# A given order of TensorE steps, loads and score sessions, two pairs a transposing bank, and one float of each row of w_in read into a scratch tile

## The chip, the core and the metric

The kernel runs on one NeuronCore of a Trainium2 chip. The metric is the device time of one execution in microseconds; the time before is the median of three runs. A profile of one further execution, taken by the hardware profiler, gives the spans of instructions on the five engines (PE is TensorE, DVE VectorE, ACT ScalarE, POOL GpSimd, SP SyncE), the landings of DMAs and the clock that PE was granted.

## What is computed

Causal attention over 4 batches, 8 heads, 768 positions and head size 64, followed by a gated feed-forward product. Three heads (0, 2 and 6) see all earlier positions; the five others see the first four positions (sinks) and a window of 64.

```python
scores = scale * np.matmul(q, k.transpose(0, 1, 3, 2))
causal = rel >= 0
is_sink = pos[None, :] < int(n_sink)
in_win = (rel >= 0) & (rel < int(window))
stream_keep = causal & (is_sink | in_win)
...
a = a / (np.sum(a, axis=-1, keepdims=True) + 1e-09)
return np.matmul(a, v).astype(np.float32)
...
x = np.ascontiguousarray(attn_out.transpose(0, 2, 1, 3)).reshape(B * S, H * D)
...
h = x @ w_in
g = h * (1.0 / (1.0 + np.exp(-beta * h)))
return (g @ w_out).astype(np.float32)
```

x has 3072 rows of 512, w_in is 512 x 2048, w_out is 2048 x 512; inputs and output are float32, the products run in bf16.

## The kernel before

The rows are cut into eight chunks of 384: chunk 2b is the first half of batch b, chunk 2b + 1 the second. A chunk goes through these steps, named as the planner names them:

- **Loads** (`load_hw`, `load_sw`, `load_v`, `load_rows`). K, Q and V of a chunk. Two loads each on SP and ACT bring the first heads of chunk 0 as float32; all others, and w_in and w_out in four pieces each, go through POOL's queue, which casts to bf16. `ORDER` names the order of the loads of w_in, w_out and chunks 1 and 2 behind those of chunk 0 ("k1a" is K of chunk 1, heads 0 to 3, "b" heads 4 to 7, "v10" a third of V of chunk 1).
- **Transposes of K and Q**. For chunks 0 to 2 (`BY_HAND_C = 3`) PE transposes them (`keys_ramp`, L542), one pair of heads to a PSUM bank, and DVE or ACT copies the bank to KT or QT (`copy`, L385). From chunk 3 on SP issues DMA transposes (`keys_rows`, L556).
- **Scores** in sessions (`session`, L689). A session fills some banks with blocks of 128 x 128; two heads run side by side in the upper and lower 64 rows of the array. ACT then takes the exponential of each bank into es (L698). Chunk 0's masks are added on PE as products with the identity (L674); the other chunks' masks are multiplied in on DVE (L718, L722). Copies of K and V blocks for the sinks (KO, VO) are made on POOL or DVE.
- **Probabilities times V** (L742), the reciprocal of the sums (L745) and the division into x (L752), all four pairs of heads.
- **Transposes of x** (`x_transposed`): on PE for chunks 0 to 3 and 7 (L764), with a copy to xT by DVE or ACT; as four DMA transposes on SP (L770) for chunks 4, 5 and 6.
- **First product** (`first_part`, L784): 16 groups of four matmuls of 384 columns, xT against w_in; ACT takes the tanh (th, L787) and DVE makes gT from it (gate, L789). A group's bank is held until DVE has read it.
- **Second product** (`second_part`, L804): three row tiles of 16 matmuls of 512 columns, gT against w_out; ACT or DVE copies the bank out (osb) and SP stores it. The last row tile is cut into two halves of 256 columns, each copied and stored in two quarters.

There are eight PSUM banks for all of it. All instructions are emitted by a planner (`Plan.run`), which replays the kernel with assumed costs and takes, on each engine, the task that can start first; the table of PE's lanes ("F1" first product, "F2" second product, "S" sessions) sets the order of these on PE, and all other PE tasks go ahead of them when ready. Before, that table came from `STAGE_0` for chunk 0 and from the function `stage`, which spreads both products evenly between sessions. Every engine executes its instructions in the order in which they were emitted. `fill` puts matmuls of zeros (L968) into waits of PE in the first 16 us of the plan; eight more (L448) stand at the very beginning.

Of the kernel before, what the change touches and what calls it, by code (L numbers as in the profile page):

```python
# [8 lines left out]
F32 = mybir.dt.float32  # L9
# [46 lines left out]
class Task:  # L56
    __slots__ = ("name", "alts", "deps", "prio", "emit", "take", "drop", "mode", "load", "n_wait", "after",
                 "done", "start", "engine", "seq", "follow", "lane")
# [11 lines left out]
class Rings:  # L70


    LAND = 1100.0

# [5 lines left out]
    def add(self, queue, task, ready, work, packet):  # L80
        self.queues[queue].append([task, ready, work, packet])

    def step(self, until):
# [11 lines left out]
        for q in self.queues.values():  # L95
            if q and q[0] in live and q[0][2] <= 1e-3:
                h = q.pop(0)
                self.landing.append((self.now + self.LAND, h[0].seq, h[0]))
                self.landing.sort()
# [19 lines left out]
class Plan:  # L119
# [6 lines left out]
    PATIENCE = 150.0  # L126

# [11 lines left out]
    def run(self, key, ahead):  # L139
# [48 lines left out]
        while left:  # L188
# [65 lines left out]
            t.start, t.engine = now, e  # L254
# [4 lines left out]
            if t.load is not None:  # L259
                kind, delay, work, packet = t.load  # L260
                rings.add(e, t, now + delay, work, packet)
# [19 lines left out]
    def let_go(self, h, at):  # L281
        h.users -= 1
        h.until = max(h.until, at)
        if h.users == 0:
# [7 lines left out]
FILL_END, FILL_SPARE = 16000.0, 120.0  # L292
BY_HAND_C = 3
AHEAD = 8
STAGE_0 = [(3, 0, 0), (3, 0, 1), (3, 0, 2), (3, 0, 3), (4, 0, None)]
SESSIONS = {0: [(3, 3), (3, 3)], 1: [(4, 3), (4, 3), (3, 3)]}
SESSIONS_1 = [(3, 2), (3, 2), (3, 3), (2, 2)]
# [4 lines left out]
def XT_PE(c, m):  # L302
    return c < 4 or c == 7
# [3 lines left out]
def kernel(  # L307
# [13 lines left out]
    nc = tc.nc  # L321
# [131 lines left out]
    PACKET = {256: 18.3, 768: 37.0, 2048: 78.0, 512: 27.0}  # L453
    seq, chain = [0], []

    def dma(name, queue, issue, size, count, deps, fn, take=(), drop=(), prio=None, follow=()):
# [3 lines left out]
        if queue == "POOL":  # L460
            follow, chain[:] = list(follow) + chain, []
        delay = issue + 700.0 if queue == "POOL" else max(issue, 460.0) + 640.0
        t = P.add(name, [(queue, issue, 0.0)], deps, seq[0] * 0.001 + (prio or 0), lambda _: fn(eng[queue]), take, drop,
                  load=(kind, delay, PACKET[size] * count, PACKET[size]), follow=follow)
# [68 lines left out]
    def keys_ramp(c, p):  # L533
        for name, holder, made in (("k", KH, GK), ("q", QH, GQ)):
            src = [QK[name, c, h] for h in PAIR[c][p]]
            bank = Hold(BANKS)

            def tr(_, bank=bank, src=src):
                tp = bank.buf.bitcast(BF16)[:, 0:HALF].rearrange("p (t j) -> p t j", t=HT)
                for t in range(HT):  # L540
                    for a, (_, hold, i) in enumerate(src):
                        nc.tensor.transpose(tp[half(a), t, :], hold.buf[:, i, t], ident)  # L542
            t = P.add(f"T{name}{c}.{p}", [pe(384, 3)], [x[0] for x in src] + [t_id], c * 100 + p * 10, tr, take=[bank], drop=[x[1] for x in src])

            def ev(e, bank=bank, holder=holder):
                tp = bank.buf.bitcast(BF16)[:, 0:HALF].rearrange("p (t j) -> p j t", t=HT)
                copy(e, holder[c].buf[:, p].rearrange("p (j t) -> p j t", t=HT), tp)
            made[c, p] = [P.add(f"E{name}{c}.{p}", [dve(384), act(384)] if c or p < 2 else [dve(384)], [t], c * 100 + p, ev, take=[holder[c]], drop=[bank])]
# [102 lines left out]
    def session(c, parts, prio, lane):  # L651
# [13 lines left out]
        by_pe = c == 0  # L665
# [11 lines left out]
        def go(_):  # L677
# [12 lines left out]
            for a, lo, part, bank in work if by_pe else []:  # L690
                if not retr[part[0][0]] and len(part) == 2:
                    nc.tensor.matmul(bank.buf[0:sink_i, 0:128], KH[f].buf[half(a), WHERE[c][part[0][0]][1], 0:sink_i], QH[c].buf[half(a), WHERE[c][part[0][0]][1], 256:384], start=True, stop=True)  # L692
        occ = max(time) / 2.4 + 5.0 * count + (sum(time) / 2.4 + 97.0 if by_pe else 0.0)
# [10 lines left out]
    def masks_and_products(c, pairs):  # L704
# [3 lines left out]
        for h in range(H):  # L708
            at, lst = PLACE[c, h]
            if c == 0:  # L710
                made[h] = []
                continue
            prio = c * 100 + 10 * WHERE[c][h][1] + 1
# [298 lines left out]
```

## Time and profile before

| | |
|---|---|
| runs | 234.52 us median (233.3, 234.52, 235.13) |
| the profiled execution | 234.75 us; span from its first to its last instruction 232.8 us |
| granted PE clock, mean | 0.991 |
| busy: PE, ACT, DVE, POOL | 221.4, 151.9, 142.0, 92.0 us |
| first product, 512 matmuls | 94.7 us busy |
| second product, records of 379 of its 400 matmuls | 89.0 us busy |
| tanh on ACT, 128 | 74.6 us busy |
| exponentials on ACT, 132 | 61.3 us busy |
| DMA | 25.77 MB in 92488 packets; POOL's queue 72.0% of 16 engines' span |

A row of the groups names the line, engine and operation, what it writes and reads, and the count; then the busy time in us and the mean ns of one; then the engine's idle time ahead of them and what ended it. The chain that ended last is followed back from the last instruction, at each step to what released it or to the instruction before it on its engine. In the table of stages each engine has its busy time and, in brackets, its instructions. Matmuls are pipelined, so the duration of one exceeds the distance from one to the next; the distance is what PE pays.

### The profile page before, as it was taken

To read this page: it belongs to the slowest core of one execution; us is meant where nothing else is said; L and a number is where in the kernel's file an instruction comes from. 1 tells how busy PE (TensorE), PEld (TensorE's weight loads), DVE (VectorE), ACT (ScalarE), POOL (GpSimd) and SP (SyncE) were. 2 spreads that over 40 slices of the span, in tenths; PEclk is the share of its full clock that TensorE was granted. 3 is DMA by queue.
4 is the path that set the end of the run, shared out by engine and by line. 5 is a ranking of instruction groups with operands and counts; after the bars stand their busy time and mean duration, and the time that the engine had idled before them with its cause. 6 is when DMAs were issued, how large, how long until landed. Compare 5 with 4: busy or idle time off the path is not lost.

```text
span 232.8 us, 5227 instructions
## 1 busy us (share of the span) xinstructions
PE 221.4 (95%) x1967; PEld 127.1 (55%) x1988; DVE 142.0 (61%) x353; ACT 151.9 (65%) x299; POOL 92.0 (40%) x141
## 2 busy tenths in 40 slices
PE   7999689999599999999999999999999999999993
PEld 3465466545365565655555556555655656555453
DVE  5666598655795666876775466674847458434321
ACT  3767998526569687776667876965676876555300
POOL 8948543698999834898600004100000000000000
PEclk9999999999799999999999999999999999999999
DMA  7999999999999999999992114311220110111112
GB/s 168 162 197 204 182 207 196 137 128 170 157 157 164 155 196 111 132 139 136 196 167 68 48 34 114 82 28 55 62 62 3 45 48 1 45 47 46 45 45 90
DMA packets 92488, 25.77 MB, mean 111 GB/s; under 512 B 83872, under 2 KB 89520, under 8 KB 92464
## 3 DMA queue, kind: packets, MB, share of 16 engines
q0 software_dynamic: 66144, 13.24, 72.0%
q1 hardware_dynamic: 25456, 11.67, 23.3%
q10 hardware_dynamic: 864, 0.53, 0.7%
q8 instruction: 15, 0.25, 0.4%
q14 instruction: 9, 0.07, 0.1%
HBM read 27.27 MB, written 6.29 MB: 144 GB/s over the span
## 4 chain that ended last, share of the span: by engine, by line
PE 90%; ACT 4%; DVE 3%; issue 1%
PE bank L804 36%; PE bank L784 35%; PE bank L689 6%; PE bank L742 5%; ACT es L698 4%; PE bank L542 2%; PE bank L764 2%; PE bank L448 2%; PE bank L674 1%; PE bank L968 1%; DVE gT L789 1%; DVE es L722 1%; DVE x L752 0%; PE bank L692 0%; DVE KO L385 0%
## 5 line engine op out<-in xcount | busy, mean ns | idle before, releaser
L787 ACT ACTIVATE th<-bank,beta_h 128x384 f32<-128x384 f32 x128 | 74.6, 592 | 40.9 <-PE bank L784 34.6
L784 PE MATMUL bank<-xT,w_in_sb 128*128 128x384 bf16 x512 | 94.7, 328 | 0.1
L804 PE MATMUL bank<-w_out_sb,gT 128*128 128x512 bf16 (+1 forms) x379 | 89.0, 372 | 1.4 <-issue 0.3
L789 DVE SCALAR_TENSOR_TENSOR gT<-th,bank 128x384 bf16<-128x384 f32 x128 | 69.3, 549 | 27.8 <-ACT th L787 24.5
L698 ACT ACTIVATE es<-bank 128x512 bf16<-128x512 f32 (+3 forms) x132 | 61.3, 585 | 16.3 <-PE bank L689 16.3
L784 PEld LDWEIGHTS <-w_in_sb 128*128 128x128 bf16 x512 | 48.3, 98 | 33.9 <-issue 1.2
L804 PEld LDWEIGHTS <-gT 128*128 128x128 bf16 x400 | 37.8, 98 | 38.4 <-issue 2.0
L722 DVE TENSOR_TENSOR es<-es,M 128x768 bf16<-128x768 bf16 (+1 forms) x35 | 18.3, 527 | 18.4 <-ACT es L698 18.0
L497 POOL DMA_DIRECT2D VX<-in_v_dram x24 | 21.4, 915 | 8.2 <-DMA w_out_sb<-in_moe_w_out_dram 4.9
L519 POOL DMA_DIRECT2D kr<-in_k_dram x30 | 22.6, 795 | 3.6 <-DMA w_out_sb<-in_moe_w_out_dram 1.7
L519 POOL DMA_DIRECT2D qr<-in_q_dram x30 | 22.3, 762 | 1.6 <-DMA kr<-in_k_dram 0.8
L689 PE MATMUL bank<-QT,KT 64*128 64x128 bf16 (+2 forms) x281 | 19.8, 241 | 1.8 <-ACT es L698 1.5
L742 PEld LDWEIGHTS <-es 128*128 128x128 bf16 x472 | 17.6, 97 | 5.0 <-issue 0.9
L742 PE MATMUL bank<-VX,es 128*128 128x65 bf16 x392 | 18.8, 193 | 0.3 <-DVE es L722 0.3
L385 POOL COPY KO<-KT 128x128 bf16<-128x128 bf16 (+3 forms) x24 | 6.9, 325 | 30.4 <-PE bank L689 22.9
L816 ACT ACTIVATE osb<-bank 128x512 f32<-128x512 f32 (+1 forms) x17 | 9.5, 560 | 13.5 <-DVE osb L818 9.9
L689 PEld LDWEIGHTS <-KT 64*128 64x128 bf16 x281 | 12.3, 94 | 9.9 <-issue 8.5
L752 DVE TENSOR_TENSOR x<-bank,rec 128x384 bf16<-128x384 f32 x32 | 17.3, 550 | 0.5
L818 DVE TENSOR_SCALAR osb<-bank 128x512 f32<-128x512 f32 (+1 forms) x10 | 6.1, 611 | 16.8 <-PE bank L804 16.7
L718 DVE TENSOR_TENSOR es<-es,Mc 128x384 bf16<-128x384 bf16 x21 | 7.4, 352 | 5.5 <-ACT es L698 5.5
L745 DVE RECIPROCAL rec<-bank 128x6 f32<-128x6 f32 x32 | 6.1, 193 | 7.4 <-PE bank L742 5.7
L742 PE MATMUL bank<-VO,es 128*128 128x65 bf16 x80 | 9.9, 193 | 0.6 <-DVE gT L789 0.5
(60 smaller groups left out, 111.8 us busy)
## 6 DMA issues: line engine op xcount, KB each, us to landing
out_dram<-osb SPq DMA_DIRECT2D x23, 256.0 KB, 2.2
VX<-in_v_dram POOLq DMA_DIRECT2D x24, 128.0 KB, 6.1
w_in_sb<-in_moe_w_in_dram POOLq DMA_DIRECT2D x4, 512.0 KB, 11.5
w_out_sb<-in_moe_w_out_dram POOLq DMA_DIRECT2D x4, 512.0 KB, 13.8
kr<-in_k_dram POOLq DMA_DIRECT2D x30, 64.0 KB, 5.6
qr<-in_q_dram POOLq DMA_DIRECT2D x30, 64.0 KB, 4.5
qkb<-in_k_dram POOLq DMA_DIRECT2D x5, 192.0 KB, 10.9
qkb<-in_q_dram POOLq DMA_DIRECT2D x5, 192.0 KB, 11.2
```

The source lines that it names most:

```text
L497: LD["v", c, t] = dma(f"ldv{c}.{t}", "POOL", 1000, 256, 64, list(deps) + [t_ones[id(x)] for x in V_r.names], lambda e: e.dma_start(out=VH[ ...
L519: ROW[name, c, t] = [dma(f"row{name}{c}.{t}.{a}", "POOL", 750, 256, 32, [], lambda e, t=t, a=a, r=r, i=i, src=src: e.dma_start(out=hold.bu ...
L689: nc.tensor.matmul(bank.buf[:, place * 128:(place + n) * 128], kk[1](), QH[c].buf[half(a), WHERE[c][h][1], i * 128:(i + n) * 128], start=n ...
L698: x = P.add(f"exp{c}.{a}.{lo}", [act(w * 128)], [t], prio, lambda _, e0=e0, w=w, bank=bank: nc.scalar.activation(out=EH[c].buf[:, e0 * 128 ...
L722: made[h] = [P.add(f"mask{c}.{h}", [dve(n * 128, 0.53)], list({EXPS[c, at + i] for i in range(n)}) + [t_mask], prio, lambda _, n=n, m0=m0, ...
L742: nc.tensor.matmul(view()[:, i, a, 0:D + 1], EH[c].buf[:, e0 * 128:(e0 + 1) * 128], val(), start=(j == 0), stop=(j == len(mine) - 1))
L752: nc.vector.tensor_mul(xo, view()[:, :, :, 0:D], rec.buf.to_broadcast([128, HT, 2, D]))
L784: nc.tensor.matmul(bank.buf[:, 0:HALF], w_in_sb[:, mo, fi * 128:(fi + 1) * 128], XTH[c].buf[:, mo, :], start=(mo == 0), stop=(mo == MO - 1))
L787: t = P.add(f"th{c}.{fi}", [act(HALF, 97)], [t, t_beta], c * 100, lambda _, fi=fi, bank=bank, th=th: nc.scalar.activation(out=th.buf, in_= ...
L789: GATE[c, fi] = P.add(f"gate{c}.{fi}", [dve(HALF)], [t], c * 100, lambda _, fi=fi, bank=bank, th=th: nc.vector.scalar_tensor_tensor(out=GH ...
L804: nc.tensor.matmul(bank.buf[:, 0:hi - lo], GH[c].buf[:, fi, ns * 128:(ns + 1) * 128], w_out_sb[:, fi, lo:hi], start=(fi == 0), stop=(fi == ...
L816: nc.scalar.activation(out=osb.buf[:, 0:h - l], in_=src, func=ACTF.Copy, scale=0.5)
```

## The change

The planner's constants, its order of lanes and loads, and parts of the emission change; what is computed does not.

- The PE lanes follow a table, `STEPS`, one letter for each task ("1" a group of the first product, "2" four matmuls of the second, "S" a session); `STAGE_0` and `stage` go. The sizes of the sessions are given for each chunk.
- The loads have another order: K of chunk 1 and half its Q stand ahead of w_in.
- For chunks 1 and 2 two pairs of heads are transposed into one bank and copied out as one instruction of 768 columns; chunk 0 keeps one pair.
- Chunk 0's pair 1 has its masks multiplied on DVE (four instructions) in place of four products on PE.
- x is transposed on PE for chunks 0 and 7 alone; chunks 1 to 6 use DMA transposes on SP.
- The first four groups of chunk 0's first product are cut into three matmuls and one, the ones behind all the threes.
- The last row tile is cut 256/128/128, one copy and store each.
- Ahead of beta's load SP issues one DMA that reads one float of each row of the four blocks of w_in, 512 in all, into a tile that nothing reads.
- Filling on PE has a rule that emits fewer of these matmuls. The planner's assumed costs and landings of DMAs change, and DVE and ACT choose with a bias for each kind of task.

```diff
+XT_PE = {0, 7}
+ADDED = {0, 2, 3}
+HEAD_PARTS = 4
+ORDER = ["k1a", "k1b", "q1a", "wi0", "wi1", "wi2", "q1b", "wi3", "wo0", "wo1", "k2a", "v11", "v12", "v10",
+         "q2b", "q2a", "k2b", "wo2", "wo3", "v20", "v22", "v21"]
-ORDER = ["wi0", "wi1", "k1a", "q1a", "k1b", "q1b", "wi2", "wi3", "v10", "v11", "v12", "wo0", "wo1", "wo2", "wo3",
-         "k2a", "k2b", "q2a", "q2b", "v20", "v21", "v22"]
+STEPS = ("1111111211112111S11111S112S11211111221S2112S1111S1221212212121111111S111122222S21122"
...
-    def keys_ramp(c, p):
+    def keys_ramp(c, ps):
...
+                tp = bank.buf.bitcast(BF16)[:, 0:n * HALF].rearrange("p (g t j) -> p g t j", t=HT, g=n)
...
-        by_pe = c == 0
+        by_pe = c == 0 and WHERE[c][heads[0]][1] in ADDED
...
-            if XT_PE(c, m):
+            if c in XT_PE:
...
+            parts = [order[:-1], order[-1:]] if c == 0 and fi < HEAD_PARTS else [order]
...
-            for lo, hi in (((0, 256), (256, 512)) if last else ((0, 512),)):
+            for lo, hi in (((0, 256), (256, 384), (384, 512)) if last else ((0, 512),)):
...
+    touched = sb([128, MO, 1], F32, "touched")
+    dma("touch", "SP", 470, 4, 32, [], lambda e: e.dma_start(out=touched, in_=moe_w_in.rearrange("(mo mi) f -> mi mo f", mi=128)[:, :, 0:1]), prio=-400)
...
-        for p in range(NP):
-            keys_ramp(c, p)
+        for ps in ([(p,) for p in range(NP)] if not c else [(0, 1), (2, 3)]):
+            keys_ramp(c, ps)
...
+    lanes = {"1": [t for c in range(NC) for t in F1[c]], "2": [t for c in range(NC) for t in F2[c]], "S": [t for c in range(1, NC) for t in SES[c]]}
+    P.script = [lanes[x].pop(0) for x in STEPS]
```

On PE, where chunk 0's x has been transposed, the order before reads (x_105 is x of chunk 0, xT_107 its transpose, qkb_77 K of chunk 1):

```order
L764 LDWEIGHTS x_105
L764 MATMUL bank_69<-idb,x_105 128x128
...
L968 LDWEIGHTS zeros
L968 MATMUL bank_68<-zeros 128x256
...
L784 LDWEIGHTS w_in_sb
L784 MATMUL bank_64<-xT_107,w_in_sb 128x384
...
L542 LDWEIGHTS qkb_77
L542 MATMUL bank_65<-idb,qkb_77 64x128
```

and now, with KT_90, QT_96 and KO_93 being K, Q and sink blocks of chunk 1, KT_89 K of chunk 0 and qkb_80 the second half of chunk 1's Q:

```order
L795 LDWEIGHTS x_105
L795 MATMUL bank_68<-idb,x_105 128x128
L705 LDWEIGHTS KT_90
L705 MATMUL bank_65<-QT_96,KT_90 128x256
L705 LDWEIGHTS KO_93
...
L705 MATMUL bank_70<-QT_96,KT_89 128x128
L819 LDWEIGHTS w_in_sb
L819 MATMUL bank_68<-xT_107,w_in_sb 128x384
...
L555 LDWEIGHTS qkb_80
L555 MATMUL bank_64<-idb,qkb_80 64x128
```

Chunk 1's first transposes stood behind three groups of chunk 0's first product; now all but the last step of them, and a session of seven banks, stand ahead of it.

On ACT, at chunk 1's exponentials (es_104) and chunk 0's tanh (th), before:

```order
L787 ACTIVATE th_113<-bank_68,beta_h 128x384
L385 COPY QT_96<-bank_69 128x384
L698 ACTIVATE es_104<-bank_63 128x512
L698 ACTIVATE es_104<-bank_64 128x512
...
L698 ACTIVATE es_104<-bank_68 128x512
L787 ACTIVATE th_114<-bank_63,beta_h 128x384
```

and now:

```order
L394 COPY xT_107<-bank_70 128x384
L714 ACTIVATE es_104<-bank_65 128x512
...
L714 ACTIVATE es_104<-bank_70 128x512
L825 ACTIVATE th_112<-bank_68,beta_h 128x384
...
L825 ACTIVATE th_116<-bank_70,beta_h 128x384
L714 ACTIVATE es_104<-bank_64 128x512
L714 ACTIVATE es_104<-bank_68 128x512
```

Sixteen exponentials stood in a row behind seven of the sixteen tanh; now seven come first, then fifteen tanh, then five and eight with one tanh between.

On SP, from its beginning, before (kr and qr are rows of K and Q of chunks 3 and up, KT_92 and QT_96 those of chunk 3):

```order
L480 DMA ld_72<-in_k_dram 128x2x192
L480 DMA ld_74<-in_k_dram 128x2x192
L556 DMA_TRANSPOSE KT_92<-kr_85 128x4x128 x3
L821 DMA out_dram<-osb_117 128x512
L556 DMA_TRANSPOSE QT_96<-qr_86 128x4x128 x3
```

and now, with xT_108 and xT_109 for chunks 1 and 2:

```order
L491 DMA ld_72<-in_k_dram 128x2x192
L491 DMA ld_74<-in_k_dram 128x2x192
L873 DMA touched<-in_moe_w_in_dram 128x4x1
L801 DMA_TRANSPOSE xT_108<-x_106 128x3x128 x4
L859 DMA out_dram<-osb_117 128x512
...
L572 DMA_TRANSPOSE KT_92<-kr_85 128x4x128 x3
L801 DMA_TRANSPOSE xT_109<-x_105 128x3x128 x4
L572 DMA_TRANSPOSE QT_96<-qr_86 128x4x128 x3
```

The transposes of x of chunk 1 now head SP's queue behind the first loads, and those of chunk 2 stand between K and Q of chunk 3.

More of the change, by code (lines that the diff above doesn't have):

```diff
@@ L70 @@
 class Rings:
-    LAND = 1100.0
     def __init__(self):
@@ L253, in run @@
                     self.mode = t.mode
-            t.start, t.engine = now, e
+                if now < self.WARM and t.name != "idle":
+                    occ, lat = 2 * occ, lat + occ
+            t.start, t.engine, t.occ = now, e, occ
             free[e] = now + occ
@@ L259, in run @@
             if t.load is not None:
-                kind, delay, work, packet = t.load
-                rings.add(e, t, now + delay, work, packet)
+                kind, delay, work, packet, land = t.load
+                rings.add(e, t, now + delay, work, packet, land)
                 sent[kind].append(t)
```

164 lines of the change are left out of this document (79 added, 85 removed).

## The prediction

> **What bounds the kernel now.** First the busy shares of the page, its chain that ended last, and then the table of stages, cut where the character of the work changes (columns: us; busy us of PE, PEld, DVE, ACT and POOL; granted clock; DMA share; GB/s).
>
> ```profile
> span 232.8 us, 5227 instructions
> PE 221.4 (95%) x1967; PEld 127.1 (55%) x1988; DVE 142.0 (61%) x353; ACT 151.9 (65%) x299; POOL 92.0 (40%) x141
> PE 90%; ACT 4%; DVE 3%; issue 1%
> ...
> 17.30:24.70 7.40, 7.40 (x93) 4.44 (x91) 5.40 (x12) 5.44 (x12) 5.95 (x14) 1.00 1.41 199
> 24.70:33.00 8.30, 6.25 (x98) 4.23 (x96) 5.25 (x12) 8.30 (x19) 4.14 (x6) 1.00 1.55 194
> 53.90:61.30 7.40, 4.88 (x68) 3.20 (x69) 6.01 (x19) 4.75 (x10) 6.66 (x11) 1.00 1.86 172
> 61.30:64.80 3.50, 3.17 (x17) 1.55 (x17) 2.22 (x5) 2.59 (x7) 3.50 (x5) 0.51 1.98 128
> 121.80:171.40 49.60, 49.28 (x427) 28.27 (x433) 31.36 (x69) 35.52 (x68) 4.29 (x9) 1.00 0.24 61
> ```
>
> PE is busy 95% and carries 90% of the chain, so only two things can shorten the kernel: less PE work, or fewer stretches in which PE waits. From 64.8 us on there are hardly any. The waits stand early. From 24.7 to 33.0 us ACT is busy 8.30 of 8.30 us and PE is not: chunk 1's four score sessions are issued together, and their exponentials run in one string. From 53.9 to 61.3 us chunk 2's sessions are alone at the head of the order, PE is busy 4.88 of 7.40 us, and then the granted clock falls to 0.51 for 3.5 us, which costs 1.7 us more. These are the rows of the timeline:
>
> ```profile
> 24.69 7.95 ACT L698 ACTIVATE es<-bank 128x512 bf16<-128x512 f32 x16
> ...
> 54.30 3.04 ACT L698 ACTIVATE es<-bank 128x512 bf16<-128x512 f32 x6 [4.86 <-PE bank L689]
> 60.45 0.51 PE L764 MATMUL bank<-idb,x 128*128 128x128 bf16 x6 [2.08 <-DVE x L752]
> ```
>
> One exponential of 512 columns takes 7.95/16 = 0.50 us; ACT had idled 4.86 us before the second string, and PE then idled 2.08 us for chunk 2's x. The clock drop fits the Trainium skill, "TensorE: Matmul & The Clock Gate", Part 1, by which an idle window of about 3.4 us halves PE's clock; the trace agrees (3.5 us at 0.51).
>
> The steady part gives the prices of PE work, from the chain in order of time (start, us, what):
>
> ```profile
> 121.77 0.98 PE bank L689 x17
> 122.75 1.83 PE bank L804 x8
> 125.88 0.86 PE bank L804 x4
> 131.06 0.99 PE bank L689 x17
> 133.87 0.65 PE bank L784 x4
> 139.21 0.66 PE bank L689 x15
> 142.35 0.90 PE bank L742 x30
> 147.73 0.77 PE bank L689 x16
> 171.42 0.98 PE bank L689 x17
> ```
>
> First product (L784) 0.65 us for four matmuls, second product (L804) 0.86 for four and 0.1 more right behind a session, probabilities times V (L742) 0.030 a block, the three sessions of an odd chunk 0.98 + 0.99 + 0.66 = 2.63, the two of an even one 0.77 + 0.66 = 1.43. Two chunks come to 20.8 + 20.6 + 3.5 + 4.1 + 0.5 = 49.5; the rows at 121.77 and 171.42 are 49.65 apart. So that stretch is PE work to within 0.3%.
>
> Where the kernel stands when the second chunk's first product begins, and where PE ends:
>
> ```profile
> 22.55 0.46 PE bank L542 x12
> 40.30 1.46 PE bank L804 x6
> 41.76 1.30 PE bank L784 x8
> 43.92 0.79 PE bank L542 x24
> 95.49 0.42 PE bank L764 x6
> 217.95 11.28 PE bank L804 x68
> ```
>
> PE's last matmul ends at 229.2 us; 3.5 us of eviction and store follow, and the profiled execution took 234.75 us in all, 1.95 beyond its span.
>
> **The change part by part.** *Up to the first product.* Three of chunk 1's four transposing steps and its first session (7 of 20 banks of scores) now precede chunk 0's first product, which began at 17.5 us. Of the loads, three of 192 KB now stand ahead of w_in.
>
> ```profile
> 17.52 1.95 PE bank L784 x12
> ...
> L502 POOL DMA_DIRECT2D w_in_sb<-in_moe_w_in_dram x4: 745/771/814, 6.7 to 11.9; - x4
> ...
> DMA to landing us min/median/max: 7.8/11.5/14.7
> ...
> 6.69 1.51 POOL L502 DMA_DIRECT2D w_in_sb<-in_moe_w_in_dram  x2
> ...
> w_in_sb<-in_moe_w_in_dram POOLq DMA_DIRECT2D x1, 512.0 KB, 9.9
> ```
>
> The first piece of w_in lands at 6.7 + 7.8 = 14.5, the second (issued at 7.4) at 17.3, the last at 11.9 + 14.7 = 26.6. In the 12.1 us between first and last come three pieces of w_in and four of 192 KB, 2304 KB: 2.7 us for a piece, 1.0 for a small one. With 3.0 us more ahead of it the first piece lands at 17.5, when the session that stands ahead of the product on PE (0.99) has not begun: no wait there, and a piece each 2.7 us keeps up with its 16 matmuls (2.6 us). The evictions of two pairs at once, 768 columns, have no row:
>
> ```profile
> L385 DVE COPY KT<-bank 128x384 bf16<-128x384 bf16 x8 | 4.2, 552 | 3.0 <-PE bank L542 3.0
> L818 DVE TENSOR_SCALAR osb<-bank 128x512 f32<-128x512 f32 x8 | 5.5, 691 | 14.3 <-PE bank L804 14.2
> ```
>
> At 0.139 us per 128 columns one takes 0.97 against two at 1.10, bounded by 0.69 and 1.10. It saves little, but one of them now stands on DVE between two of chunk 0's x (before, none), and the masks of pair 1 move there as well: I take 0.45 us, bounds 0 and 1.0. Session 1.0 starts at 17.8. Four mask matmuls and twelve filling matmuls fewer lie where PE waits for data: nothing. But filling keeps PE busy, and PE starts slow:
>
> ```profile
> 1.30 3.60 PE bank L448 x8
> ```
>
> That is 0.45 us for 512 columns against 0.215 in the steady part. If full pace came one window of 3.5 us later (the length of the drop above), PE would lose at most 1.7 us; most of that hides behind evictions, so I take 0 and keep 1.7 for the range.
>
> *The touch.* One DMA of 512 floats on SP, behind the two loads and ahead of nothing until 38 us. Its price is bounded by 0 and by the pace of the queue's packets, 232.8 x 16 x 0.233 / 25456 = 34 ns, or 512 x 34 / 16 = 1.1 us of all DMA engines; its gain by 0 and about 0.3 (w_in's second piece landed 2.8 us behind the first, 0.1 over the mean, and the first may hold twice as much). Either ends before session 1.0 does, which covers it: 0.
>
> ```profile
> q1 hardware_dynamic: 25456, 11.67, 23.3%
> ```
>
> The Trainium skill, "DMA: Bandwidth & Descriptors", Rules for kernel authors, speaks against it: a pattern without contiguous elements becomes one descriptor per element. No run here shows that for four bytes; by the rule the sum would take the 1.1 at worst.
>
> *From 17.8 us to chunk 1's first product.* The new order puts all of this in between: session 1.0 (0.99), the first product of chunk 0 (64 matmuls, 10.4), 12 transposes (0.46), sessions of 16, 17 and 5 matmuls (0.77 + 0.98 + 0.4), the second product of chunk 0 (48, 10.3), chunk 1's 75 blocks (2.25), chunk 2's 48 transposes (1.6) and both its sessions (1.65): 29.8, with switches 30.0. ACT's part until chunk 1's last block is 20 exponentials and 16 tanh:
>
> ```profile
> L787 ACT ACTIVATE th<-bank,beta_h 128x384 f32<-128x384 f32 x128 | 74.6, 592 | 40.9 <-PE bank L784 34.6
> ```
>
> 20 x 0.50 + 16 x 0.58 = 19.3 us within 21: close, but no longer the bound, since the tanh now run between exponentials. I allow 1.0 for waits (bounds 0 and 5): chunk 0's second product holds three of eight banks until w_out is in, so sessions wait for banks. First product of chunk 1: 17.8 + 30.0 + 1.0 = 48.8. Before, it stood at 41.8, but with 40 of those second-product matmuls (8.6), 48 transposes (1.6) and chunk 2's sessions (1.4) still to come, so 53.4 at like work: 4.6 gained.
>
> *Transposes of x.* 36 of the 60 leave PE (0.42/6 = 0.07 each, 2.5 us; 0.8 of it before the point above) and become 12 DMA transposes on SP, for chunks 1 to 3, while loads run.
>
> ```profile
> xT<-x SPq DMA_TRANSPOSE x4, 5.2
> xT<-x SPq DMA_TRANSPOSE x8, 2.4
> L770 SPq DMA_TRANSPOSE xT<-x x12: 1180/1247/2093, 104.6 to 167.8; - x12
> ...
> DMA to landing us min/median/max: 2.4/5.2/7.6
> ```
>
> The first two lines are the four issued from 90 to 126 us, under loads, and the eight behind; the last is that of the K and Q transposes (L556). Four issues of 1.25 and a landing of 5.2 give 9.0 us from the first issue to the last landing. Chunk 1 has 9.0 us of PE work ahead of its first product (transposes 1.6, 24 matmuls 5.2, sessions 1.65, rest switches), chunk 2 has 7.8 + 2.6 = 10.4. Behind chunk 2's four in SP's queue stand the Q transposes of chunk 3; they have the 7.2 us of the next first product as cover. From chunk 3 on an attention stage lies between. I take 1.0 for chunk 2 (0 to 4) and 1.0 for its 32 blocks, which wait for seven exponentials right behind the session (3.5 + a mask 0.55 against 3.0 of PE work).
>
> *Rest.* First product 448 matmuls, 72.8; second 336, 72.2; 354 blocks, 10.6; sessions of chunks 3, 5, 7 and 4, 6, 7.9 + 2.9 + 1.3 behind them; 12 transposes of x, 0.8: 168.5. The last quarter store is split 256/128/128 in place of twice 256: the same 128 columns are evicted last, 0. Sum: 48.8 + 168.5 + 2.0 + 3.5 = 222.8 of span, + 1.95 = 224.75 us against 234.75 of that execution, which is 0.23 above the median of 234.52. I forecast **224.8 us**, 4% faster.
>
> **Rivals.** (1) *Banks and ACT still bind from 29 to 48 us*: sessions of 5, 5 and 3 banks must wait in turn because three banks are held, and each exponential's 0.50 is paid; 24 to 33 us speaks for it, ACT's 19.3 of 21 leaves room against it. Price 4 to 5: 229. (2) *Late transposes*: at the worst rows (2.09 an issue, 7.6 to land) the chain is 13.9 us, 4.9 beyond chunk 1's cover and 3.5 beyond chunk 2's, less the 2 allowed: 231. (3) *The other side: slower.* The same chain when x, K, Q and loads meet on SP and in the DMA engines: both first products wait, chunk 3's sessions wait behind them for Q, and each wait past 3.4 us brings a clock drop of 1.7 as at 61.3. Each us of landing beyond 7.6 costs two, so it decides from about 9 us on: at 10 us 4.8 more than (2) and 3.4 of clock, 239. For it speaks that w_in took 14.7 us behind other loads; against it that no K or Q tile took over 7.6. (4) *The waits only move*, since the order is written for durations that the chip need not keep: the 24.7 to 33 and 53.9 to 65 losses (about 2 and 5) return elsewhere, and only the 2.5 of the transposes is kept: 232.3 to 234.
>
> **How the numbers follow.** Forecast 0.60, (1) 0.14, (2) 0.12, (3) 0.06, (4) 0.08. A measurement tells 1% from no change, 232.2 and 236.9 being the bounds: faster 0.60 + 0.14 + 0.12 = 0.86, same 0.08, slower 0.06. The range runs from 220.5 (the 3.0 of waits gone, and a ramp 1.3 shorter: no delay of x, and evictions at their lower bound) to 231.5, which takes in (1) and (2) and leaves out (3), (4) and a little of the forecast on both sides.
>
> **What would show it.** Right: chunk 1's first product begins at 47 to 50 us; no stretch with ACT at 100% and PE below 80%; granted clock 1.00 from 7 to 229 us; 24 DMA transposes of x, 24 on PE; the steady part again 49.6 us for two chunks. Wrong: PE waiting on a DMA of xT or QT for over 2 us, an idle stretch over 3 us, or a first product of chunk 0 later than 20 us, which would put the blame on w_in's place in the loads.

## The result and the profile after

The changed kernel takes 232.97 us (median of 20 runs, 231.53 to 235.78) against 234.65 us of the kernel before on the same chip (20 runs). The ratio is 0.994, with a 95% interval of 0.992 to 0.9961: 0.6% faster, within the 1% that the prediction counted as no change, where 224.8 us and a range of 220.5 to 231.5 had been forecast. The profiled execution took 231.53 us.

The page of the changed kernel, its busy shares and its chain that ended last:

```profile
span 229.6 us, 5164 instructions
PE 219.2 (95%) x1952; PEld 125.5 (55%) x1952; DVE 143.2 (62%) x349; ACT 145.8 (64%) x284; POOL 92.9 (40%) x143
PE 82%; DMA 11%; DVE 3%; SPq 1%; issue 1%; ACTq 0%; ACT 0%; POOL 0%
```

PE is as busy as before, 95%, though 36 transposes have left it. The chain tells what has changed: before, DMA was not in it, now it carries 11%. The table of PE's waits names the transfer (columns: us in all, times, longest):

```profile
PE bank L819 <- DMA xT<-x: 5.9, 6, 3.0
...
```

Only the wait for the first zeros at the start (1.3 us) and one of 0.2 for beta stand below it: behind the start there is one cause, the first product (L819) waiting six times for transposed x, 5.9 us in all. Where that is, and what follows, stands in the table of stages (columns as in the prediction):

```profile
17.60:28.00 10.40, 10.40 (x75) 6.05 (x74) 8.16 (x17) 9.95 (x21) 4.68 (x8) 1.00 1.28 205
28.00:39.00 11.00, 11.00 (x162) 6.97 (x163) 7.12 (x18) 7.25 (x17) 7.34 (x9) 1.00 1.65 188
39.00:46.58 7.58, 7.58 (x90) 4.15 (x86) 4.74 (x14) 5.45 (x10) 3.06 (x7) 1.00 1.87 149
46.58:50.00 3.42, 1.55 (x17) 0.68 (x13) 1.82 (x4) 2.90 (x7) 2.53 (x4) 1.00 1.80 184
50.00:53.41 3.41, 3.41 (x22) 1.89 (x20) 2.56 (x7) 1.31 (x3) 2.47 (x4) 0.50 1.98 270
...
63.00:66.60 3.60, 3.05 (x15) 1.31 (x14) 1.24 (x3) 0.38 (x1) 3.60 (x5) 1.00 2.11 183
...
101.19:104.61 3.42, 2.06 (x31) 1.26 (x29) 2.63 (x11) 2.78 (x6) 1.16 (x4) 1.00 2.23 160
104.61:108.02 3.41, 1.19 (x7) 0.63 (x7) 0.51 (x2) 0.44 (x1) 1.44 (x3) 1.00 1.55 177
108.02:111.43 3.41, 3.41 (x13) 1.56 (x12) 1.91 (x5) 1.89 (x4) 0.43 (x1) 0.50 1.91 200
111.43:226.70 115.27, 115.21 (x908) 66.15 (x906) 66.23 (x139) 68.80 (x130) 10.42 (x18) 1.00 0.30 59
```

The stretches that the prediction was most worried about, 17.6 to 46.6 us, have no wait at all: PE is busy 10.40 of 10.40, 11.00 of 11.00 and 7.58 of 7.58 us. Chunk 1's first product is reached at 46.9 us, and there PE is busy 1.55 of 3.42 us, followed by a stretch at a granted clock of 0.50. Chunk 2 waits about 0.5 us between 63 and 66.6 us. Chunk 3 waits 3.6 us between 103 and 107 us, again with a half-clock stretch behind it. From 111 us on PE never stops. The last transfers in the chain, in order of time (start, us):

```profile
41.87 7.82 DMA xT<-x
60.59 5.92 DMA xT<-x
99.83 7.29 DMA xT<-x
```

These are the fourth transposes of chunks 1, 2 and 3. What SP issued ahead of the last one (start, us of issue):

```profile
89.93 4.51 SPq L572 DMA_TRANSPOSE QT<-qr  x3
95.01 1.20 SPq L572 DMA_TRANSPOSE KT<-kr  x1
96.33 0.51 SPq L859 DMA_DIRECT2D out_dram<-osb  x1
96.96 1.31 SPq L572 DMA_TRANSPOSE KT<-kr  x1
98.36 2.73 SPq L801 DMA_TRANSPOSE xT<-x  x2
```

Chunk 3's last x was written at 95.50 us. Its transposes were issued at 98.36 and 99.83, because SP works in order and two K transposes of chunk 6 and a store stood ahead.

### The profile page after: what moved, and what is told of

It is laid out like the page before. It is cut to its first block, busy times and chain, and to the rows that moved or that the text cites. A ratio compares the mean times of both kernels' runs of the same rounds, so it can differ in the third digit from the quotient of the medians.

```text
span 229.6 us, 5164 instructions
## 1 busy us (share of the span) xinstructions
PE 219.2 (95%) x1952; PEld 125.5 (55%) x1952; DVE 143.2 (62%) x349; ACT 145.8 (64%) x284; POOL 92.9 (40%) x143
## 4 chain that ended last, share of the span: by engine, by line
PE 82%; DMA 11%; DVE 3%; SPq 1%; issue 1%; ACTq 0%; ACT 0%; POOL 0%
PE bank L819 34%; PE bank L842 32%; DMA xT<-x 9%; PE bank L705 7%; PE bank L773 6%; DMA beta_r<-in_moe_beta_dram 2%; PE bank L555 2%; DVE gT L827 1%; PE bank L690 1%; SPq L801 1%; PE bank L795 1%; DVE x L783 1%; ACTq L491 0%; DVE osb L856 0%; DVE KO L394 0%
## 5 line engine op out<-in xcount | busy, mean ns | idle before, releaser
L819 PE MATMUL bank<-xT,w_in_sb 128*128 128x384 bf16 x512 | 93.1, 334 | 6.0 <-DMA xT<-x 5.9
L825 ACT ACTIVATE th<-bank,beta_h 128x384 f32<-128x384 f32 x128 | 73.0, 597 | 36.4 <-PE bank L819 31.0
L842 PE MATMUL bank<-w_out_sb,gT 128*128 128x512 bf16 (+2 forms) x416 | 90.8, 363 | 0.0
L827 DVE SCALAR_TENSOR_TENSOR gT<-th,bank 128x384 bf16<-128x384 f32 x128 | 67.9, 552 | 30.8 <-ACT th L825 25.9
L819 PEld LDWEIGHTS <-w_in_sb 128*128 128x128 bf16 x512 | 50.0, 100 | 42.2 <-issue 10.5
L753 DVE TENSOR_TENSOR es<-es,M 128x768 bf16<-128x768 bf16 (+1 forms) x35 | 17.6, 520 | 8.8 <-ACT es L714 8.7
L856 DVE TENSOR_SCALAR osb<-bank 128x512 f32<-128x512 f32 (+2 forms) x17 | 11.1, 652 | 17.7 <-PE bank L842 16.6
L705 PEld LDWEIGHTS <-KT 64*128 64x128 bf16 x281 | 13.1, 94 | 9.4 <-issue 8.4
L854 ACT ACTIVATE osb<-bank 128x512 f32<-128x512 f32 (+1 forms) x9 | 5.1, 562 | 14.9 <-PE bank L842 14.9
L705 PE MATMUL bank<-QT,KO 64*128 64x128 bf16 x75 | 9.8, 217 | 0.0
```

The lines of the kernel that those rows point to most:

```text
L705: nc.tensor.matmul(bank.buf[:, place * 128:(place + n) * 128], kk[1](), QH[c].buf[half(a), WHERE[c][h][1], i * 128:(i + n) * 128], start=n ...
L753: made[h] = [P.add(f"mask{c}.{h}", [dve(n * 128, 0.53)], list({EXPS[c, at + i] for i in range(n)}) + [t_mask], prio, lambda _, n=n, m0=m0, ...
L819: nc.tensor.matmul(bank.buf[:, 0:HALF], w_in_sb[:, mo, fi * 128:(fi + 1) * 128], XTH[c].buf[:, mo, :], start=(mo == order[0]), stop=(mo == ...
L825: t = P.add(f"th{c}.{fi}", [act(HALF, 97)], [t, t_beta], c * 100, lambda _, fi=fi, bank=bank, th=th: nc.scalar.activation(out=th.buf, in_= ...
L827: GATE[c, fi] = P.add(f"gate{c}.{fi}", [dve(HALF)], [t], c * 100, lambda _, fi=fi, bank=bank, th=th: nc.vector.scalar_tensor_tensor(out=GH ...
L842: nc.tensor.matmul(bank.buf[:, 0:hi - lo], GH[c].buf[:, fi, ns * 128:(ns + 1) * 128], w_out_sb[:, fi, lo:hi], start=(fi == 0), stop=(fi == ...
```

## The experiments

All ratios below are to the kernel before on the same chip. Theory A: the waits for the DMA transposes of chunks 1 to 3, with the two half-clock stretches, ate the gain. Rival B: they come from the order of steps and would move elsewhere. In most experiments the planner, run again, moves other steps on PE as well. In 12 and 13 it does not: PE executes the same instructions in the same order as in 10 and in the change, so these two are the cleanest.

| kernel | us | ratio (95%) |
|---|---|---|
| the change | 232.97 | 0.994 (0.992 to 0.9961) |
| 1: x of chunks 1, 2, 3 on PE | 228.43 | 0.976 (0.97 to 0.9819) |
| 2: x of chunk 3 on PE | 228.16 | 0.9729 (0.9676 to 0.9782) |
| 3: loads held | 227.42 | 0.9722 (0.9664 to 0.978) |
| 4: no touch | 233.27 | 0.9951 (0.992 to 0.9982) |
| 5: as 1, no late filling | 226.79 | 0.9695 (0.9648 to 0.9741) |
| 6: as 5, chunk 2 by DMA | 228.25 | 0.9734 (0.9672 to 0.9795) |
| 7: before, chunks 2 and 3 by DMA | 232.62 | 0.9927 (0.9899 to 0.9955) |
| 8: as 5, one pair a bank | 226.29 | 0.9703 (0.9626 to 0.9779) |
| 9: transposes on two queues | 249.52 | 1.0651 (1.0593 to 1.071) |
| 10: as 5, chunk 3 by DMA | 231.3 | 0.987 (0.9805 to 0.9934) |
| 11: as 10, loads of chunk 5 held | 232.03 | 0.9911 (0.9877 to 0.9945) |
| 12: as 10, chunk 3's x ahead on SP | 226.59 | 0.9666 (0.9647 to 0.9685) |
| 13: the change, chunk 3's x ahead on SP | 230.04 | 0.9814 (0.9776 to 0.9852) |

### 1 and 2: the transposes back on PE

```diff
-XT_PE = {0, 7}
+XT_PE = {0, 1, 2, 3, 7}     (experiment 1)
+XT_PE = {0, 3, 7}           (experiment 2)
```

> x of chunks 1, 2 and 3 is transposed on PE again (36 transposes, 0.07 us each: 2.5 us more PE work), all else of the change stays. Theory A (PE's waits of 2.8, about 1 and about 5 us for the DMA transposes of x, and the two clock drops of 1.7 us that follow them, are where the forecast gain went): 12 us of waits and clock go, 2.5 of work comes, so 9 to 10 us less than the changed kernel, about 223 to 226 us, with no wait of PE for xT over 1 us and a granted clock of 1.00 from 7 us on. Rival B (the waits come from the order of steps, the banks or ACT, and xT only happens to arrive last): PE then waits for something else at the same places and the time stays within 2 us of 233.

> Only chunk 3's x is transposed on PE again (12 transposes, 0.8 us). Theory A: of the waits only those of chunk 3 go (3.6 us of idle PE in the stage from 97.3 to 107.2, about 1 before it, 1.7 of clock), less 0.8: 4 to 6 us less than the changed kernel, 227 to 229 us; the wait for chunk 1's xT near 47 us (2.8) and its clock drop near 50 us stay as they are. Rival B: the wait near 100 us stays, ended by something else, and the time is unchanged.

With all three on PE the chain is PE's again, and no wait for xT is left:

```profile
span 225.7 us, 5256 instructions
PE 95%; DMA 2%; DVE 1%; issue 1%; SPq 0%
```

The time falls to 0.976, 4.2 us (0.018 of 234.6) below the change: A's sign, and half of its size. With chunk 3 alone on PE it falls as far. Chunks 1 and 2 still wait there, and the clock stays at 1.00:

```profile
PE bank L819 <- DMA xT<-x: 3.2, 3, 1.3
```

So B falls, and chunk 3 carries most. Not all of the 4.95 us (0.0211 of 234.6) is chunk 3's, though: the drop near 50 us, which was expected to stay, did not come in this execution. What was missing in the first is looked for in the fifth.

### 3: loads held behind the transposed x

The loads of K, Q and V of chunk c+2 wait, for c from 1 to 5, until a small copy on GpSimd has read the transposed x of chunk c.

```diff
+        if 1 <= c <= NC - 3:
+            held = sb([128, MO, 1], BF16, f"held{c}")
+            g = P.add(f"hold{c}", [pool(4)], [XTD[c, m] for m in range(MO)], ..., nc.gpsimd.tensor_copy(out=held, in_=XTH[c].buf[:, :, 0:1]), drop=[XTH[c]])
+            for t in [...loads of chunk c + 2...]:
+                t.deps.append(g)
```

> The DMA transposes of x stay, but a small copy on GpSimd that reads the transposed x of chunk c-2 stands ahead of the loads of K, Q and V of chunk c+2 ... that is, for c from 1 to 5 the loads of chunk c+2 wait for the transposed x of chunk c. Theory A1 (the landings of 7 to 8 us come from the loads that run beside them): the transposes of chunk 2 and 3 land in 2.4 to 5 us, those of chunk 1 too if the loads that now wait are the ones that ran then; 3 to 8 us less than the changed kernel, unless the late loads make sessions wait. Theory A2 (the landing is slow by the order of SP's queue or by the transposes among themselves, whatever the loads do): landings stay at 6 to 8 us and the time within 2 us of 233 or above.

The landings of x issued from 90 to 100 us (count, median us), and what PE waits for in the whole run:

```profile
xT<-x SPq DMA_TRANSPOSE x4, 3.1
```

```profile
PE bank L705 <- DMA QT<-qr: 2.2, 1, 2.2
...
PE bank L819 <- DMA xT<-x: 0.7, 1, 0.7
```

The wait for xT falls from 5.9 to 0.7 us, and the time by 5.1 us (0.994 to 0.9722 of 234.6). A new wait for Q, 2.2 us, takes part of it back: the loads that were held are now the late ones. Chunk 1's landings moved less: its x took 5.3 to 8.5 us, in the change 6.9 to 8.3, though the K loads of chunk 3, issued there from 36.26 us on, were held until 48.64. That was enough: the last landed at 48.08 us in place of 49.69, and PE, which began chunk 1's first product at 47.51, did not wait. The gain is smaller by a half-clock stretch behind the wait for Q (120.22 to 123.63 us) and by 23 filling matmuls at 121 to 125 us, which the new plan put there.

### 4: without the touch

```diff
-    touched = sb([128, MO, 1], F32, "touched")
-    dma("touch", "SP", 470, 4, 32, [], ...)
```

> The DMA that reads one float of each row of w_in is taken out; nothing else moves. The step of the prediction (it costs and gains nothing): within 0.5 us of the changed kernel, every first load 0.15 to 0.5 us earlier (K of chunk 0 lands at 6.55 in place of 7.02 us). Rival (the touch warms the path to w_in): the first pieces of w_in land later by up to 1 us without it, session 1.0 (16.6 us) stays and the first product of chunk 0 starts later than 17.6 us, time up to 1 us longer.

The time differs by 0.1%, inside the interval. The landings do move. The median of w_in's four pieces and the begin of the first product, first with the touch, then without:

```profile
w_in_sb<-in_moe_w_in_dram POOLq DMA_DIRECT2D x4, 512.0 KB, 10.8
```

```profile
17.57 0.99 PE L819 MATMUL bank<-xT,w_in_sb 128*128 128x384 bf16 x5
```

```profile
w_in_sb<-in_moe_w_in_dram POOLq DMA_DIRECT2D x4, 512.0 KB, 11.4
```

```profile
18.00 0.50 PE L819 MATMUL bank<-xT,w_in_sb 128*128 128x384 bf16 x2
```

In these two executions w_in lands 0.6 us sooner with the touch and the first product starts 0.43 us sooner. Of that nothing that could be measured reached the end: the prediction's 0 stands. Without it the four first loads landed 0.1 to 0.3 us sooner, about as expected, but the piece of K of chunk 0 on POOL's queue, which was expected at 6.55, did not (7.24 us against 7.02).

### 5, 6 and 8: no filling, chunk 2 alone, one pair a bank

The first experiment's plan held 28 filling matmuls at 57 and 79 us that the change does not have.

```diff
-FILL_END, FILL_SPARE, FILL_MIN = 16000.0, 120.0, 1000.0
+FILL_END, FILL_SPARE, FILL_MIN = 16000.0, 120.0, 1e9       (5, 6, 8)
+XT_PE = {0, 1, 3, 7}                                       (6)
-        for ps in ([(p,) for p in range(NP)] if not c else [(0, 1), (2, 3)]):
+        for ps in [(p,) for p in range(NP)]:                (8)
```

> x of chunks 1, 2 and 3 on PE as in the first experiment, and no filling matmuls behind 16 us: the first experiment's plan had put 28 of them (3.25 us of PE, at 57 and 79 us) in places where the changed kernel has none. Theory A (the filling matmuls stood where PE had work, so they were pure loss): 3 us less than the first experiment's 228.4, about 225.2 us, and no gap of PE over 0.5 us behind 17 us. Rival C (they filled real waits): PE waits there, time 228 us.

> As the one before, but chunk 2's x by DMA transposes (12 transposes off PE, 0.8 us). Theory A (a DMA transpose issued in the loaded stretch lands 6 to 8 us later, and chunk 2's first product has less cover than four issues and such a landing): PE waits 1 to 2 us for xT near 65 us, so 0.2 to 1.2 us slower than its neighbour, 225.5 to 226.5 us. Rival: chunk 2's transposes are covered, 0.8 us faster, 224.4 us.

> As the first of this group, with one pair of heads in a transposing bank for chunks 1 and 2, as before the change; the planner's order of the steps around it moves with it. The prediction's step (two pairs in one eviction save 0.13 us each and delay x by 0.45): within 1.5 us of its neighbour's 225 us. Rival (two pairs a bank carry the gain of the first 50 us): chunk 1's first product at 45 us or later in place of 42.7, and 2 to 4 us slower.

Without the filling the span falls only from 225.7 to 225.2 us, and the ratio by 0.0065, 1.5 us (the intervals overlap): real waits of 1.1 us for banks stood in that place,

```profile
PE bank L705 <- DVE gT L827: 0.7, 2, 0.5
PE bank L705 <- ACT osb L854: 0.4, 1, 0.4
```

so the expected 3 us was a miss; how much of the filling was free, these intervals don't tell. The fifth kernel is the change without its DMA transposes of chunks 1 to 3, in the order that the planner makes of that: 0.9695. Between it and the change lie 0.0245 of 234.6, 5.7 us, and that is what the DMA transposes cost, net of the 2.5 us of work that they take off PE.

With chunk 2 alone by DMA, its x was ready later than in the change (issues from 66.9 to 70.9 us, first product at 74.1), PE waited 3.2 us and lost a stretch of clock:

```profile
74.00:78.10 4.10, 0.88 (x11) 0.36 (x8) 1.78 (x6) 0.20 (x1) 2.81 (x4) 0.97 2.38 163
78.10:81.50 3.40, 3.40 (x16) 1.88 (x16) 1.11 (x2) 1.42 (x3) 2.38 (x4) 0.54 1.58 202
```

That wait is longer than the 1 to 2 us expected. The ratio is 0.9734 against 0.9695, 0.9 us slower, with overlapping intervals: the sign is A's, but it isn't shown by the times. Its x was written at 64.75 us, so here too SP issued it 2.2 us late.

One pair a bank gives 0.9703 against 0.9695: no difference, as the prediction's step had it. Chunk 1's first product began at 41.65 us, not at 45 or later (43.17 with two pairs), so the rival falls. The planner moved other steps with it, so this bounds the pair banks together with that.

### 7: that part of the change alone, in the old order

```diff
 def XT_PE(c, m):
-    return c < 4 or c == 7
+    return c in (0, 1, 7)
```

> The kernel before, with the x of chunks 2 and 3 by DMA transposes in place of PE: that part of the change alone, in the old order. Theory A: chunk 2's x is ready at 69.2 us and chunk 3's at 95.3, first products at 74.0 and 100.5; two issues (2.5) and a landing of 6 to 8 us bring xT at 78 to 80 and 104 to 106, so PE waits 4 to 5 us twice, less 1.6 of transposes taken away, and 1.7 more for each clock drop: 4 to 11 us slower than before, 239 to 245 us. Rival B (DMA transposes of x are covered in any order, the waits of the changed kernel come from its order of steps): 1.6 us faster, 233 us.

Here A's numbers failed: 1.7 us faster (0.0073 of 234.5), as much as the 1.6 that left PE, as the rival said. PE waits 1.3 us once, for chunk 2:

```profile
PE bank L784 <- DMA xT<-x: 1.3, 1, 1.3
```

Chunk 3's transposes were issued at 94.65 and 95.88 us, the first 0.03 us behind its last x (94.62); those issued from 94 to 101 us landed in 4.2 us (median), where those of the change issued from 96 to 101 took 7.6:

```profile
xT<-x SPq DMA_TRANSPOSE x2, 4.2
```

```profile
xT<-x SPq DMA_TRANSPOSE x2, 7.6
```

So a DMA transpose of x under loads is not late in every order. It is late in the change's order, where it is issued late and into a fuller stretch: the DMA share from 86 to 96 us is 1.36 in this run,

```profile
86.00:96.00 10.00, 9.90 (x102) 5.84 (x101) 8.42 (x26) 7.24 (x15) 4.85 (x8) 1.00 1.36 158
```

and 1.96 in the change (PE busy throughout):

```profile
86.00:96.00 10.00, 10.00 (x111) 5.74 (x110) 6.81 (x23) 6.06 (x13) 6.84 (x11) 1.00 1.96 175
```

Theory A was narrowed by this to two suspects for chunk 3: SP's order (A-queue) and the loads in flight (A-load).

### 9: two issuing queues

```diff
-                XTD[c, m] = dma(f"Xx{c}.{m}", "SP", ...
+                XTD[c, m] = dma(f"Xx{c}.{m}", "ACT" if c <= 3 and m % 2 else "SP", ...
```

> The changed kernel with every second DMA transpose of x of chunks 1, 2 and 3 issued by ACT in place of SP (six of twelve); all else as it was. Theory A-queue (the four issues of 1.2 to 2.1 us stand behind one another and, for chunk 3, behind K and Q transposes and stores on SP, and that is a large part of the wait): the last issue comes 2 to 3 us earlier for each chunk, the waits of 1.6, about 1 and 3.6 us shrink by as much, the clock drops go, 5 to 8 us less than the changed kernel, 225 to 228 us. Theory A-load (the landing takes what the DMA engines need, whichever queue issues): the last landing comes less than 1 us earlier and the time within 2 us of 233, with 1.2 us of ACT for each issue lost besides.

It told neither apart. In the program each transpose of one queue waits until that of the other has landed. In the trace ACT waits for the semaphore of SP's transpose, and the two queues take turns: SP's first transpose of chunk 1 landed at 45.05 us and ACT's was issued at 45.13, that one landed at 48.35 and SP's second was issued at 48.45. All that stood behind the transpose on ACT stopped:

```profile
45.13 1.28 ACTq L801 DMA_TRANSPOSE xT<-x  x1
46.45 0.80 ACT L394 COPY KT<-bank 128x768 bf16<-128x768 bf16 x1 [9.22 <-issue]
```

PE in turn waited 10.4 us for exponentials, and the kernel took 249.5 us. The Trainium skill, "DMA: Bandwidth & Descriptors", Silent corruption: two transposing streams in flight at once, says that transposes of two streams must be kept apart by a wait for the earlier one's completion; the program holds such waits, and 0.08 us from landing to issue is what they look like. No run here has two such streams in flight at once.

### 10, 11 and 12: chunk 3 alone

From experiment 5, with chunk 3's x by DMA (10); with the loads of chunk 5 held behind it as in 3 (11); or with SP's order changed and nothing else (12).

```diff
-XT_PE = {0, 1, 2, 3, 7}
+XT_PE = {0, 1, 2, 7}            (10, 11, 12)
-    for t in P.run(key, AHEAD):
+    plan = list(P.run(key, AHEAD))
+    later = [t for t in plan if t.name in ("Xk6.0", "Xk6.1")]
+    plan = [t for t in plan if t not in later]
+    at = next(i for i, t in enumerate(plan) if t.name == "Xx3.3") + 1
+    plan[at:at] = later
+    for t in plan:
         t.emit(t.engine)         (12)
```

> As the fifth experiment (x of chunks 1, 2, 3 on PE, no filling behind 16 us: 226.8 us), but chunk 3's x alone by DMA transposes. Theory A: of the 6.2 us between that kernel and the changed one, chunk 3 carries most (the run with only chunk 3 on PE was 4.8 faster than the changed kernel): 3 to 5 us slower than its neighbour, 230 to 232 us, with PE waiting 3 us or more for xT near 100 us. Rival: the three chunks' waits come from one another (a wait at chunk 1 pushes the rest), so chunk 3 alone is covered: 226 to 227 us.

> As its neighbour (chunk 3's x alone by DMA transposes), with the loads of chunk 5 held behind the transposed x of chunk 3 by a small copy on GpSimd. Theory A-load: with fewer loads beside them the transposes of chunk 3 land in 2.4 to 5 us in place of 6 to 8, and the wait near 100 us shrinks by 2 us or more: 226 to 229 us, unless chunk 5's sessions now wait for K or Q. Theory A-queue: landings as before, time unchanged or slower than its neighbour.

> As the run with chunk 3's x alone by DMA transposes (231.3 us), with one change in SP's order: two K transposes of chunk 6, which stood ahead of the last two transposes of chunk 3's x, are issued behind them. No other engine's order moves. Theory A-queue (chunk 3's x was ready at 95.4 us and its transposes were issued at 97.6 and 99.0 because of what stood ahead on SP): they are issued 1.5 to 2 us earlier, the wait of 3.9 us near 104 us falls to 2 to 2.4, and the clock drop behind it goes if the wait is under 3.4: 1.5 to 3.7 us faster than its neighbour, 227.5 to 230 us. Theory A-load (the DMA engines are the limit, an earlier issue only waits longer): landings of 8 to 10 us in place of 8, time 231 us as its neighbour.

Chunk 3 alone costs 0.987 less 0.9695, 4.1 us. Two of the four runs of 10 had no half-clock stretch (clock 1.00 throughout) and still took 229.87 and 231.08 us. In the profiled one its last x is written at 95.40 us. SP's issues from there, PE's wait, and the stage behind it:

```profile
94.25 2.65 SPq L572 DMA_TRANSPOSE KT<-kr  x2
...
97.63 2.65 SPq L801 DMA_TRANSPOSE xT<-x  x2
```

```profile
PE bank L819 <- DMA xT<-x: 3.9, 2, 3.3
```

```profile
108.00:111.50 3.50, 3.50 (x15) 1.78 (x14) 1.60 (x4) 1.74 (x3) 3.34 (x4) 0.61 1.80 180
```

With chunk 5's loads held, x issued from 90 to 100 us lands in 2.4 us (median), not 8.1, and PE does not wait for it. But PE waits 3.3 us for Q instead, and the time is no better: 0.9911.

```profile
xT<-x SPq DMA_TRANSPOSE x3, 2.4
```

```profile
PE bank L705 <- DMA QT<-qr: 3.3, 1, 3.3
```

With two K transposes of chunk 6 behind x instead of ahead:

```profile
96.83 2.57 SPq L801 DMA_TRANSPOSE xT<-x  x2
99.56 4.90 SPq L572 DMA_TRANSPOSE KT<-kr  x3
```

```profile
PE bank L819 <- DMA xT<-x: 1.1, 1, 1.1
```

x of chunk 3 (written at 96.80 us here) is issued at once and lands in 7.2 and 7.4 us, its neighbour's in 8.3 and 7.9. From the writing of x to its last landing it takes 8.7 us in place of 11.4; 2.2 of the 2.7 us between are SP's queue, 0.5 the landing. PE waits 1.1 us in place of 3.9, with no half-clock stretch behind. The ratio goes from 0.987 to 0.9666: 4.8 us, more than the 3.7 expected at most. That kernel is as fast as the one with chunk 3 on PE (experiment 5), and of all tried here the one with the lowest ratio. (Its profiled execution began chunk 0's first product at 19.64 us, its neighbour's at 17.68, with a full clock from 10.51 us on, its neighbour's from 4.95, so their spans, 226.5 and 229.3, show less than the medians.) So in this place the load makes the landing 7 us long, and the order of SP's queue decides whether 7 us is too long.

### 13: the same edit in the changed kernel

> The changed kernel whole, with nothing but two K transposes of chunk 6 issued on SP behind the last two transposes of chunk 3's x in place of ahead of them. If SP's order is what made chunk 3's x late here too: the last two are issued 2.5 us earlier than 98.4 and 99.8, PE's wait of 3.6 us at 103 to 107 falls to 1 to 1.5 and the clock drop at 108 goes: 3.5 to 5 us less than the changed kernel, 228 to 229.5 us, with the waits of chunk 1 and 2 and the drop at 50 us as they were. If the neighbour's gain came from elsewhere (its first 50 us, or chunk 1's and 2's transposes being on PE): 232 to 233 us.

The edit is that of experiment 12, in the change as it was. 0.994 goes to 0.9814, 3.0 us; expected were 3.5 to 5. The wait at chunk 3's first product is 1.1 us, and the drop at 108 us is gone, but another wait has come:

```profile
PE bank L819 <- DMA xT<-x: 2.7, 4, 1.1
PE bank L819 <- DVE gT L827: 1.9, 1, 1.9
```

```profile
109.54 0.30 DVE L394 COPY KO<-KT 128x128 bf16<-128x128 bf16 x2 [4.89 <-DMA KT<-kr]
```

DVE stood 4.89 us at a copy of chunk 6's K, which now landed at 109.52; the gates (L827) queued behind it, and PE ran out of banks. In experiment 12 the same K transposes landed at 106.4 and 107.7 us and PE waited for nothing there. PE's order being that of the change, the 3.0 us are shown to come from two transposes in SP's queue. The drop near 50 us stayed (51.05 us), as expected.

## Why the prediction was wrong, by its steps

**Up to the first product: right in kind, 1.2 us too high.** Session 1.0 began at 16.58 us, where 17.8 had been said, and the first product of chunk 0 at 17.57. No wait for w_in stood there, and the clock was full from 5.6 us on (6.7 before). An eviction of 768 columns took 0.95 us on DVE and 0.80 on ACT (0.97 predicted). The touch: 0, as measured in experiment 4.

**From 17.8 us to chunk 1's first product: right, and somewhat better.** 46.9 us against 48.8. ACT did not bind (9.95 of 10.40, then 7.25 of 11.00, PE full), so rival (1) falls; the 1.0 us of waits and the delay of x were not needed.

**Transposes of x: this step failed.** It gave 4 issues and a landing of 5.2 us, 9.0 us from the first issue to the last landing, against covers of 9.0 and 10.4, and 1.0 us of waits in all for them; for chunk 3 it said "From chunk 3 on an attention stage lies between" and priced nothing. Measured landings (count, median us, by 30 to 50, 50 to 70 and 70 to 100 us of issue):

```profile
xT<-x SPq DMA_TRANSPOSE x4, 8.1
...
xT<-x SPq DMA_TRANSPOSE x4, 6.6
...
xT<-x SPq DMA_TRANSPOSE x4, 7.1
```

The 5.2 came from transposes issued between 104 and 120 us in the kernel before, and from K and Q; the early, fuller stretch (DMA share 1.65 to 2.76 in the changed kernel) had no row of x. That is chunk 1 (11.9 us from its first issue, 37.82, to its last landing, 49.69) and, in part, chunk 2 (10.6). The dearer part is the sentence on chunk 3. The stage between was there, but its x is finished only at its end, 7.3 us before the first product (95.5 to 102.8), and SP's queue took 2.9 of these. Experiments 10 and 12 show it: with 2.2 us of that queue taken away, 4.8 us come back. Experiment 13 shows it in the change itself: 3.0 us.

**The sum.** 46.9 for 48.8; then PE work until 226.6 us, which is 179.7 less 5.9 of waits and 3.4 of half clock (two stretches of 3.41 us at 0.50), 170.4 for 168.5; waits and clock 9.3 for 2.0; a tail of 3.0 for 3.5; 1.93 outside the span for 1.95. Together 231.5 for 224.8: the 6.8 us between are 7.3 of waits and clock, 1.9 of PE work, less 1.9 and 0.5. That the two 1.9 cancel is luck: they are errors of different terms. Experiment 5 makes the same point from the other side. The sum without the DMA transposes is 224.8 + 2.5 - 1.0 = 226.3 us, and that kernel took 226.8; the size agrees, helped by this cancelling and in an order planned anew.

**The rivals.** The time fell where (4) had it, 232.3 to 234, but not by its mechanism: the losses at 24.7 to 33 and 53.9 to 65 us did not return. What happened is (2) and (3), with chances of 0.12 and 0.06: late transposes, x, K, Q and loads meeting on SP, and clock drops. (3) was priced by landings of 10 us, which no x took (8.3 at most), and so came out at 239; it needed no longer landing, only a late issue. It also tied the clock drops to waits past 3.4 us; the one at 50 us stood behind waits of at most 1.15 us. Of the signs named, the one that decided was "PE waiting on a DMA of xT or QT for over 2 us" (3.0); the period of two chunks was 46.4 us (124.80 to 171.24), not 49.6, since the order shifted work between stages (97 blocks of probabilities times V between these points, where before 118 stood).

**What stays open.** For chunks 1 and 2 issue, landing and order were not taken apart; together they cost 0.8 us by the ratios of experiments 2 and 5 (0.9729 less 0.9695), whose intervals overlap. Why the DMA engines are busier from 86 to 101 us in the change than in experiment 7 stays open as well, and so does where the 1.9 us more of PE work lie.

## What to carry to other kernels

When work moves from a busy engine to a queue, price it from the moment its input is ready to the moment its reader needs it: what stands ahead in the issuing queue, then the landing in that stretch's load, not the median of a quieter one. Here a landing of about 7 us was nearly free (PE waited 1.1 us) or cost 4 to 5 us, by whether two transposes that nobody needed yet stood ahead. And moving them behind is safe only if their own readers have slack, else the wait turns up on the next engine.

## What the runs showed of the hardware

- The granted clock fell to 0.50 for 3.41 us behind stretches in which PE was not idle throughout. PE was busy 1.55 of 3.42 us in 46.58 to 50.00 (longest gap 1.15 us) and 1.19 of 3.41 in 104.61 to 108.02 (a gap of 3.03 us began before it, at 103.25). In the kernel before it was busy 1.33 of 3.41 us ahead of the drop at 61.36, so that window was not idle either, though the prediction took it for one. The two drops of the change begin 58.02 us apart, 17 times 3.413. The Trainium skill, "TensorE: Matmul & The Clock Gate", Part 1, tells of a free-running window of 3413 ns, which agrees.
- How little work brings a drop, the traces don't settle. With 2.06 of 3.42 us (101.19 to 104.61) the clock stayed. But in experiment 13, in windows of 3.41 us counted from its drop at 51.05, the clock fell behind one with 1.99 us busy (47.64 to 51.05) and stayed behind one with 1.47 (109.08 to 112.49). The busy time of PE in the profile does not decide it alone. So the same wait can bring a drop in one execution and none in another: experiment 4, with chunk 1's longest wait at 1.32 us, had none near 50 us.
- A DMA transpose of 128x384 of x lands in 2.3 to 2.4 us when few loads are in flight (2.4 in experiment 11 from 90 to 100 us) and in 6.6 to 8.1 (medians) in the loaded stretch.
- DMA transposes that are spread over two queues, each of which waits for the other's landing, cost more than they save: 249.5 us in experiment 9. That wait is the program's; no run shows what two queues do without it.
